# A step planner that models the VectorE/GpSimd exclusion and the one holder of a PSUM bank, and cos(h) from one biased Sin

## The chip, the cores and the metric

The kernel runs on one core of one Trainium2 chip. The metric is the device time of one execution in microseconds (us), the median of the runs shown. The core has five engines that work side by side and wait for each other through semaphores: TensorE (PE in the rows, its weight loads PEld), VectorE (DVE), ScalarE (ACT), GpSimd (POOL) and SyncE (SP, which issues DMAs here). Each engine runs its own queue strictly in the order in which the program was written out.

## What is computed

The reference runs three stages on 3072 tokens of width 384 (8 heads of 48, 4 batches of 768 steps):

```python
for t in range(S):                                  # linear attention with a decayed state
    kt, vt, rt = k[:, :, t], v[:, :, t], r[:, :, t]
    cur = einsum('bhd,bhe->bhde', u[None] * kt, vt)
    y[:, :, t] = einsum('bhd,bhde->bhe', rt, state + cur)
    state = w[None, :, :, None] * state + einsum('bhd,bhe->bhde', kt, vt)
h = x @ w_in; x = (h * cos(h)) @ w_out              # dense MLP, d_ff 2048
skip = x @ w_skip > 0; e = argmax(x @ w_gate)       # 8 experts, the best one of each token
x[skip] += gate * (relu(x @ w1[e]) @ w2[e])
```

## The kernel before

The recurrence is cut into 12 chunks c of 64 steps, and each chunk into two halves h of 4 heads. All large products are made of float16 pairs (a high and a low part, three matmuls for one product), so that every operand has to be split on the elementwise engines. The program is a list of some 2,300 steps; each step is a few instructions on one engine and has a name such as `("cg", g, f)`. The names used below:

- **Attention of half (c, h).** GpSimd and VectorE prepare it: `km`, `rm` (times decay), `k1l`, `r1l`, `vl`, `knl`, `al`, `zl` (low parts, a subtraction of two SBUF tiles), `pr1`, `pr2`, `am` (the diagonal). VectorE copies the parts into block matrices: `k1b`, `vb`, `knb`, `zb`, two float16 copies each (L242). PE runs `A` (scores, 24 matmuls into `ps_a`), `Y` (output, 48 into `ps_y`) and `U` (state product, 24 into `ps_u`, which VectorE reads in `zu`).
- **Dense MLP of group g** (the 256 tokens of chunk g). `("G1", g, f)`, f = 0 to 7: 18 matmuls into one of three banks `ps_h`. Then a chain over one tile `s` of 128x512: `cn` on ScalarE (L799: h/2π rounded to an integer), `cr` on VectorE (L803: h minus that many turns), `cs` on ScalarE (L806: Sin of half the rest), `cq` (a square: on ScalarE at L813 in 83 of 96 cases, on GpSimd or VectorE at L815 in the 13 others), `cg` on VectorE (L819: (1/2 - square) times h), `ch` on ScalarE (high part) and `cl` on GpSimd (L824: low part). `("G2", g, t, q)`: 12 matmuls each into `ps_o`, for two token tiles t and four quarters q.
- **Routing of group g.** `lg` on VectorE reads the logits out of `ps_o` (L864), `ra` on VectorE makes the one-hot choice (L904 to L917, eight small instructions, the last of which writes `oh`), `rp` on PE counts (5 matmuls into `ps_u`), `rb` on VectorE makes the slot of each token (L938 to L946), `rs` on GpSimd stores the records by two indirect DMAs (L952).
- **Experts** at the end: `ws` loads, `eh2`/`el2` splits of the weights, `e1`, `e2` on PE, a gather and a scatter by GpSimd.

`ps_u` is one PSUM bank. It is used by `U`, by `rp`, by `clp` (a count at the end of group 9) and by `ovp`, and each of them has to leave it to its reader first.

The order of each engine's queue comes from the class `Plan`. `order()` plays the steps through greedy engines: at each moment an idle engine takes, among its steps whose inputs are there, the one with the lowest priority number. `add(key, engine, cost, fn, deps, prio)` gives the cost in ns (functions `c_a`, `c_v`, `c_p`), and the table `SHIFT` moves priorities of the first chunks. Only the order of the queues comes out of it; on the chip every instruction waits for its data. In this model VectorE and GpSimd never disturb each other, and the bank `ps_u` is not known to it. The step `rp` therefore carries two hand-written predecessors, `("zu", g + 2, 0)` and `("U", g + 2, 0)`.

Of the kernel before, what the change touches and what calls it, by code (L numbers as in the profile page):

```python
# [7 lines left out]
F32 = mybir.dt.float32  # L8
# [10 lines left out]
C = 64                  # chunk of the recurrence  # L19
NC = S // C             # chunks  # L20
KF = DFF // 128         # tiles of moe_d_ff
CAP = 256               # token slots of an expert outside of the overflow loop
NS = E * CAP // 128     # slot tiles
NOV = 24                # upper bound on overflow blocks
REC = 10                # words of a routing record: row of xd, row of the output, shifted logits
BIG = 1 << 20           # an id past every bound
NO = DM + 9
EARLY = [0, 2]          # slot tiles that take tokens of the groups up to GE only
GE = 9
TURN = [1, 3]           # slot tiles that the tensor engine transposes  # L30
TR = NT + 128           # records of an expert: its tokens, and those that closing a tile passes over
NF = 1                  # chunks whose attention is in float32 products
NXG = 7                 # gathered token tiles on chip
NWS = 4                 # loads of expert weights in flight

# powers of two that the float16 parts are scaled by
SR = 2.0 ** 7           # r times its decay
SK = 2.0 ** 7           # k times its decay
SA = SR * SK            # attention scores
SV = 2.0 ** 7  # L40
SKN = 2.0 ** 7          # k times its decay, for the state
SZ = SKN * SV           # state
SY = SA * SV            # = SZ * SR
# [4 lines left out]
SO = SH * SWO / 2       # cos(h) / 2 = 1 / 2 - sin(h / 2)^2  # L48
# [8 lines left out]
CF = {}                 # columns of the float constants  # L57
# [8 lines left out]
class Plan:  # L66
    """Lists single-engine steps in the order in which greedy engines would start them.

    A step has an estimate of its time, the steps it has to come after, and a priority (the lowest goes first).
    The order decides only what each engine's queue looks like; Tile waits for the data itself.  # L70
    """
# [3 lines left out]
    SELF = {"PE": 0, "V": 125, "A": 140, "P": 100}  # L75

# [6 lines left out]

    def order(self):
        left, users = {}, {}
        for k, (_, _, _, deps, _, _) in self.steps.items():
            deps = [d for d in deps if d in self.steps]
            left[k] = len(deps)
            for d in deps:
                users.setdefault(d, []).append(k)  # L90
        done, ring, rings, heat = {}, 0.0, [], 0.0
        engs = ("PE", "V", "A", "P", "Q", "N")
        ready, free = {e: [] for e in engs}, {e: self.START + 400 * (e == "A") for e in engs}
        seq = {k: i for i, k in enumerate(self.steps)}
# [4 lines left out]
        while any(ready.values()):  # L99
            at, eng = min((max(free[e], min(r for r, _ in ready[e])), i) for i, e in enumerate(engs) if ready[e])  # L100
            eng = engs[eng]
            _, _, pick = min((self.steps[k][4], seq[k], (r, k)) for r, k in ready[eng] if r <= at)
            ready[eng].remove(pick)
            k = pick[1]
            _, cost, _, _, _, nbytes = self.steps[k]
# [8 lines left out]
            if nbytes:  # L114
                # at most 8 DMAs are under way
# [11 lines left out]
            else:  # L127
                end = at + cost + self.LAT.get(eng, 0)
                free[eng] = at + cost
            out.append((at, len(out), k))  # L130
            done[k] = end, free[eng]
            for u in users.get(k, ()):
                left[u] -= 1
                if not left[u]:
# [3 lines left out]
                    ready[eu].append((t, u))  # L138
# [7 lines left out]


# The start, where the elementwise engines carry the most: shifts of priorities, the order of the pieces of w_in and
# w_out, and steps on another engine than usual.
PIECES = "iiioioioioioiooo"  # L150
PIECE_0, PIECE_STEP = -40, 8
SHIFT = {
# [1269 lines left out]
```

## Time and profile before

| | us |
|---|---|
| runs | 777.3, 778.96, 1282.4 (median 778.96) |
| the profiled execution's span | 781.2 |
| PE busy in it | 628.7 |
| DVE busy in it | 613.4 |
| ACT busy in it | 438.7 |
| POOL busy in it | 430.1 |

The steps are recorded by helpers, so a line such as L236 (every matmul) or L242 (every VectorE copy) stands for many steps, and tiles tell them apart. A matmul's row lasts longer than its share of the queue, since matmuls overlap. A VectorE or GpSimd row begins when the instruction leaves the queue: what it waits for after that is inside its duration. Waits for semaphores are shown as idle time before a row, in square brackets, with the row that ended it. For the profiled execution, the routing steps `rp` of groups 0 to 8 stand at 169.3, 220.2, 270.6, 323.2, 370.4, 416.9, 462.7, 506.0 and 545.1 us; they serve as milestones.

### The profile page before, as it was taken

Reading aid. Unit: us, or ns where it says so; the run is one execution under the profiler, and the core shown is the slowest. Engines: PE = TensorE matmul, PEld = TensorE weight load, DVE = VectorE, ACT = ScalarE, POOL = GpSimd, SP = SyncE. Lnnn points to the kernel's source line nnn. Section 1 sums busy time; section 2 is a strip of 40 time slices with the busy share of each in tenths; the row PEclk is TensorE's granted clock in tenths of the full one; section 3 lists DMA queues with packets and bytes.
Section 4 is the critical chain, followed back from the end, with each engine's and each line's share of the span. In section 5 each row is a group of like instructions: output and inputs, shape, how many; then the busy total and the mean of one; then the engine's idle time right before and its main releaser. Section 6 shows DMA issues by size and latency. Waiting matters only on the chain. (4 is left out here: it accounts for less than half of the span.)

```text
span 781.2 us, 16117 instructions
## 1 busy us (share of the span) xinstructions
PE 628.7 (80%) x6407; PEld 477.6 (61%) x6407; DVE 613.4 (79%) x1022; ACT 438.7 (56%) x743; POOL 430.1 (55%) x367
## 2 busy tenths in 40 slices
PE   3436578958779497696996969799998998998994
PEld 3434456737557375474774748577775576675672
DVE  7999999998889989787886878776576537987641
ACT  3356667777654545464655645666676524655420
POOL 6787878468777766766566666442334424222110
PEclk9998799989989799698998989999999999999997
DMA  9867535440213203122120311201077224999610
GB/s 248 241 157 219 136 81 141 132 129 24 81 52 103 76 4 108 45 68 88 46 91 21 111 44 57 76 1 47 13 239 233 71 57 112 265 293 270 222 37 16
DMA packets 64752, 86.95 MB, mean 111 GB/s; under 512 B 32878, under 2 KB 49436, under 8 KB 64674
## 3 DMA queue, kind: packets, MB, share of 16 engines
q1 hardware_dynamic: 61570, 80.56, 36.0%
q0 software_dynamic: 2816, 4.91, 2.3%
q8 instruction: 51, 0.84, 0.5%
q10 hardware_dynamic: 288, 0.43, 0.2%
q14 instruction: 27, 0.22, 0.1%
HBM read 66.57 MB, written 13.73 MB: 103 GB/s over the span
## 5 line engine op out<-in xcount | busy, mean ns | idle before, releaser
L236 PE MATMUL ps_h<-xt,wih 128*128 128x256 f16 x1152 | 210.5, 287 | 20.1 <-DVE s L819 20.1
L236 PE MATMUL ps_o<-wo,gt 128*128 128x393 f16 (+2 forms) x1200 | 209.1, 326 | 0.1
L824 POOL TENSOR_TENSOR gt<-s,gt 128x512 f16<-128x512 f32 x96 | 121.0, 1264 | 106.8 <-ACT gt L240 106.0
L236 PE MATMUL ps_h<-xt,wil 128*128 128x256 f16 x576 | 165.1, 287 | 0.0
L236 PEld LDWEIGHTS <-gt 128*128 128x128 f16 x1200 | 113.5, 99 | 73.9 <-issue 3.0
L236 PEld LDWEIGHTS <-wih 128*128 128x128 f16 x1152 | 114.0, 102 | 45.0 <-DVE s L819 19.5
L819 DVE SCALAR_TENSOR_TENSOR s<-s,ps_h 128x512 f32<-128x512 f32 x96 | 65.3, 682 | 44.2 <-ACT s L813 43.6
L803 DVE SCALAR_TENSOR_TENSOR s<-s,ps_h 128x512 f32<-128x512 int32 x96 | 65.3, 681 | 29.7 <-ACT s L799 29.5
L806 ACT ACTIVATE s<-s 128x512 f32<-128x512 f32 x96 | 60.3, 628 | 49.9 <-DVE s L803 48.7
L240 ACT ACTIVATE gt<-s 128x512 f16<-128x512 f32 x96 | 60.0, 626 | 46.2 <-DVE s L819 45.8
L236 PE MATMUL ps_o<-w,hh 128*128 128x384 f16 x384 | 67.5, 332 | 4.8 <-ACT hh L1187 2.7
L799 ACT ACTIVATE s<-ps_h 128x512 int32<-128x512 f32 x96 | 56.3, 586 | 24.3 <-PE ps_h L236 23.6
L247 DVE SCALAR_TENSOR_TENSOR w<-ws,w 128x768 f16<-128x768 f32 (+1 forms) x56 | 59.4, 1076 | 11.6 <-ACT w L240 10.5
L240 ACT ACTIVATE w<-ws 128x768 f16<-128x768 f32 (+1 forms) x56 | 51.3, 930 | 29.6 <-DMA ws<-in_w_dram 19.2
L236 PE MATMUL ps_h<-xe,w 128*128 128x256 f16 (+1 forms) x720 | 65.7, 251 | 2.6 <-issue 1.7
L236 PEld LDWEIGHTS <-wil 128*128 128x128 f16 x576 | 59.4, 103 | 9.6
L236 PEld LDWEIGHTS <-w 128*128 128x128 f16 x720 | 58.9, 98 | 9.1 <-issue 3.1
L1220 POOL DMA_INDIRECT out_dram<-xg,recs x16 | 19.0, 1185 | 72.6 <-DVE xg L1215 52.9
L236 PEld LDWEIGHTS <-hh 128*128 128x128 f16 x384 | 37.1, 99 | 32.0 <-DVE hh L1192 4.2
L952 POOL DMA_INDIRECT tab<-rec,di x24 | 25.6, 1065 | 51.3 <-DVE osum L946 27.9
L813 ACT ACTIVATE s<-s 128x512 f32<-128x512 f32 x83 | 52.1, 627 | 2.1
L236 PE MATMUL ps_u<-oh,tri 128*128 128x8 f16 x24 | 2.9, 174 | 58.8 <-DVE oh L917 58.8
(179 smaller groups left out, 1193.9 us busy)
## 6 DMA issues: line engine op xcount, KB each, us to landing
nat<-in_nat_dram SPq DMA_DIRECT2D x24, 576.0 KB, 3.8
ws<-in_w_dram SPq DMA_DIRECT2D x24, 512.0 KB, 4.4
ws<-in_w_dram SPq DMA_DIRECT2D x32, 384.0 KB, 3.7
rk<-in_rk_dram SPq DMA_DIRECT2D x24, 448.0 KB, 3.7
so<-in_w_out_dram SPq DMA_DIRECT2D x8, 768.0 KB, 8.5
si<-in_w_in_dram SPq DMA_DIRECT2D x8, 576.0 KB, 6.9
xd<-y SPq DMA_DIRECT2D x24, 192.0 KB, 2.0
out_dram<-y SPq DMA_DIRECT2D x48, 96.0 KB, 2.2
```

What stands on the lines that cost most here:

```text
L236: T.matmul(o, lhsT=l, rhs=r, start=start, stop=stop)
L240: A.activation(out=o, in_=i, func=AF.Copy, scale=scale)
L247: V.scalar_tensor_tensor(out=o, in0=x, scalar=scale, in1=hi, op0=ALU.mult, op1=ALU.subtract)
L799: A.activation(out=n, in_=d["ph"], func=AF.Copy, scale=1.0 / (TWO_PI * SH))
L803: V.scalar_tensor_tensor(out=d["s"], in0=d.pop("n"), scalar=-TWO_PI * SH, in1=d["ph"], op0=ALU.mult, op1=ALU.add)
L806: lambda: A.activation(out=d["s"], in_=d["s"], func=AF.Sin, scale=0.5 / SH), [("cr", g, f)], pr)
L813: A.activation(out=d["s"], in_=d["s"], func=AF.Square)
L819: V.scalar_tensor_tensor(out=d["s"], in0=d["s"], scalar=0.5, in1=d.pop("ph"), op0=ALU.subtract, op1=ALU.mult, reverse0=True)
L824: lambda: P.tensor_tensor(out=gt[g][1][:, 2 * f:2 * f + 2], in0=d.pop("s"), in1=gt[g][0][:, 2 * f:2 * f + 2], op=ALU.subtract), [("ch", g, ...
L952: P.indirect_dma_start(out=tab[:, :], out_offset=bass.IndirectOffsetOnAxis(ap=di[:, t], axis=0), in_=rec[:, t], in_offset=None, bounds_che ...
L1220: P.indirect_dma_start(out=out[:, :], out_offset=bass.IndirectOffsetOnAxis(ap=xo["recs"][:, s, 1:2], axis=0), in_=xs_.pop(s), in_offset=No ...
```

## The change

Every comment and docstring is dropped, which moves the line numbers. Three things change.

First, the planner. A step of VectorE that reads two SBUF tiles (or copies float16 inside SBUF) is listed in `SHARED`; it and every step of GpSimd hold a common port, one at a time. While the port is held, such a step's priority is worsened by 0.04 per ns of waiting. Steps that take the bank `ps_u` (`TAKES`) are set aside while another one holds it, until its reader has run. In return `rp` and `clp` lose their hand-written predecessors. Costs of the float16 copies get a formula of their own, `c_cp`.

Second, cos(h) is computed as sin(h - 2πn + π/2), with n = round(h/2π + 1/4). The step `cq` is gone: 83 instructions of ScalarE, 8 of GpSimd, 5 of VectorE. `cn` and `cs` get a bias, and `cg` multiplies by 1/2 and by h in the same single instruction.

Third, as all priorities and costs go through the new planner, the queues of all five engines come out in another order. The tables `SHIFT`, `ENGINE` and `PIECES` are left as they were.

```diff
+    SHARED = {"wu": 1, "wx": 1, "wv": 1, "wl": 1, "k1b": 2, "k1l": 1, "r1l": 1, "pr1": 1, "pr2": 1, "am": 1, "vl": 1,
+              "vb": 2, "knm": 1, "knl": 1, "knb": 2, "al": 1, "zl": 1, "zb": 2, "us": 1, "tabs": 10, "tkd": 4, "ra": 8,
+              "rb": 3, "el2": 1, "cq": 1, "km": 2, "rm": 1}
+    WAIT = 0.04
+    TAKES = {"U": "zu", "rp": "rb", "clp": "clv", "ovp": "ov0"}
...
-            _, _, pick = min((self.steps[k][4], seq[k], (r, k)) for r, k in ready[eng] if r <= at)
+            busy = max(0.0, port.get(eng, 0.0) - at)
+            _, _, pick = min((self.steps[k][4] + (self.WAIT * busy if self.shared(k, eng) else 0.0), seq[k], (r, k))
+                             for r, k in ready[eng] if r <= at)
             ready[eng].remove(pick)
             k = pick[1]
+            if self.takes(k):
+                held = True
+                parked += [x for x in ready["PE"] if self.takes(x[1])]
+                ready["PE"] = [x for x in ready["PE"] if not self.takes(x[1])]
...
-                end = at + cost + self.LAT.get(eng, 0)
-                free[eng] = at + cost
+                n = self.shared(k, eng)
+                if n:
+                    start = max(at, port[eng])
+                    port["P" if eng == "V" else "V"] = free[eng] = start + cost
+                else:
+                    free[eng] = at + cost
+                end = free[eng] + self.LAT.get(eng, 0)
             out.append((at, len(out), k))
             done[k] = end, free[eng]
+            if self.gives(k):
+                held = False
+                ready["PE"] += [(max(r, end), x) for r, x in parked]
+                parked = []
...
+def c_cp(n):
+    return 171 + n * 0.26
...
-            k1e, cost = pick("k1b", "V", V=2 * c_v(2 * nk, 4), A=2 * c_a(2 * nk))
+            k1e, cost = pick("k1b", "V", V=2 * c_cp(2 * nk), A=2 * c_a(2 * nk))
...
-        cb = {"A": 2 * c_a(2 * nd), "V": 2 * c_v(2 * nd, 4)}
+        cb = {"A": 2 * c_a(2 * nd), "V": 2 * c_cp(2 * nd)}
...
-            A.activation(out=n, in_=d["ph"], func=AF.Copy, scale=1.0 / (TWO_PI * SH))
+            A.activation(out=n, in_=d["ph"], func=AF.Copy, scale=1.0 / (TWO_PI * SH), bias=0.25)
...
-            lambda: A.activation(out=d["s"], in_=d["s"], func=AF.Sin, scale=0.5 / SH), [("cr", g, f)], pr)
+            lambda: A.activation(out=d["s"], in_=d["s"], func=AF.Sin, scale=1.0 / SH, bias=math.pi / 2), [("cr", g, f)], pr)
-        qe, cost = "A", c_a(512) + 140
-        if g < 3:
-            qe, cost = on(("cq", g, f), "A", A=cost, P=c_p(512), V=c_v(512))
...
-        add(("cq", g, f), qe, cost, fn, [("cs", g, f)], pr)
-        def fn():
-            V.scalar_tensor_tensor(out=d["s"], in0=d["s"], scalar=0.5, in1=d.pop("ph"),
-                                   op0=ALU.subtract, op1=ALU.mult, reverse0=True)
-        add(("cg", g, f), "V", c_v(512), fn, [("cq", g, f)], pr)
+            V.scalar_tensor_tensor(out=d["s"], in0=d["s"], scalar=0.5, in1=d.pop("ph"), op0=ALU.mult, op1=ALU.mult)
+        add(("cg", g, f), "V", c_v(512), fn, [("cs", g, f)], pr)
...
-        used = [("zu", g + 2, 0), ("U", g + 2, 0)]
         add(rkey("rp", j), "PE", 100, fn,
-            [rkey("ra", j), rkey("rb", j - 1), "cst16", "tabi", "clv" if g == GE + 1 else None] + used, pr)
+            [rkey("ra", j), rkey("rb", j - 1), "cst16", "tabi", "clv" if g == GE + 1 else None], pr)
```

What that does to the queues is shown at three places, all around the routing of group 4.

**TensorE, ahead of `rp` of group 4.** Between the last `G2` matmul of group 4 and this `rp` stood `G1` of (6, 0) and `A` of (7, 0). The rows before are the end of that `A` and the beginning of `rp`:

```order
L236 LDWEIGHTS k1bd_83
L236 MATMUL ps_a<-r_3677,k1bd_83 128x64
L236 LDWEIGHTS tri
L236 MATMUL ps_u<-oh,tri 128x8
L236 LDWEIGHTS ones
L236 MATMUL ps_u<-osum,ones 128x8
```

And now:

```order
L282 LDWEIGHTS wil
L282 MATMUL ps_h<-xt,wil 128x256
L282 LDWEIGHTS tri
L282 MATMUL ps_u<-oh,tri 128x8
L282 LDWEIGHTS ones
L282 MATMUL ps_u<-osum,ones 128x8
```

The `rp` has moved behind two more `G1` steps and a `G2` quarter: 18 `ps_h`, 12 `ps_o` and 18 `ps_h` matmuls more stand between the logits' last matmul and it. Behind it, three `G2` quarters (36 matmuls) now stand ahead of `U` of (7, 0).

**VectorE, up to the one-hot `oh` of group 4.** The rows before (`s` is the tile of the cosine, `lg` the logits):

```order
L803 SCALAR_TENSOR_TENSOR s_4443<-s_4443,ps_h_4399 128x512
L819 SCALAR_TENSOR_TENSOR s_4443<-s_4443,ps_h_4399 128x512
L803 SCALAR_TENSOR_TENSOR s_4491<-s_4491,ps_h_4452 128x512
L819 SCALAR_TENSOR_TENSOR s_4491<-s_4491,ps_h_4452 128x512
L864 TENSOR_SCALAR lg_4307<-ps_o_4372 128x9
L588 TENSOR_REDUCE cc_4445<-pr_4337 128x8
L904 TENSOR_REDUCE mx_4538<-lg_4307 128x2
L907 TENSOR_TENSOR rec_4540<-lg_4307,mx_4538 128x2x8
```

And now:

```order
L288 COPY k1bd0_83<-k1d_4309 48x16x64 x2
L900 TENSOR_SCALAR lg_4143<-ps_o_3995 128x9
L850 SCALAR_TENSOR_TENSOR s_4355<-s_4355,ps_h_4313 128x512
L288 COPY vbd0_87<-vd_4010 64x16x48 x2
L856 SCALAR_TENSOR_TENSOR s_4355<-s_4355,ps_h_4313 128x512
L596 TENSOR_TENSOR zd_4340<-zs_91,zd_4340 112x384
L634 TENSOR_REDUCE cc_4468<-pr_4365 128x8
L288 COPY zbd1_90<-zd_4340 48x16x48 x2
L940 TENSOR_REDUCE mx_4491<-lg_4143 128x2
L943 TENSOR_TENSOR rec_4493<-lg_4143,mx_4491 128x2x8
```

The last two pairs of `cr` and `cg` of the group stood back to back ahead of the logits; now one pair stands behind them, with copies of the attention in the gap. Six copies and low parts come between the logits and the routing.

**GpSimd, behind the record stores `rs` of group 4.** Before, and then now:

```order
L952 DMA tab_69<-rec_4540,di_4617 25600x10 x2
L824 TENSOR_TENSOR gt1_4513<-s_4583,gt0_4512 128x512
L550 TENSOR_TENSOR am_4722<-cfs_71,cc_4445 128x512
L824 TENSOR_TENSOR gt1_4513<-s_4643,gt0_4512 128x512
L550 TENSOR_TENSOR k1d_4700<-rk_4195,k1d_4700 112x512
```

```order
L986 DMA tab_69<-rec_4493,di_4555 25600x10 x2
L596 TENSOR_TENSOR k1d_4572<-rk_3947,k1d_4572 112x512
L860 TENSOR_TENSOR gt1_3744<-s_4223,gt0_3743 128x512
L596 TENSOR_TENSOR pr_4721<-nat_4184 128x384
L860 TENSOR_TENSOR gt1_3744<-s_4355,gt0_3743 128x512
```

Before, GpSimd prepared half (8, 1) there (`k1d`); now it prepares (7, 1), half a dozen PE steps ahead of the scores that use it, and still has the cosine tiles of group 5's last pieces (`gt1_3744`) to do.

## Rows read from the trace of the kernel before

**Rows 1.** First part of the page: engine, busy us, share of span, instructions.

```profile
PE 628.7 (80%) x6407; PEld 477.6 (61%) x6407; DVE 613.4 (79%) x1022; ACT 438.7 (56%) x743; POOL 430.1 (55%) x367
```

**Rows 2.** Waits of PE: who waited for whom, us in total, times, longest.

```profile
PE ps_u L236 <- DVE oh L917: 58.8, 8, 9.6
PE ps_h L236 <- DVE s L819: 20.1, 14, 3.3
```

**Rows 3.** Stretches: length, busy us PE, PEld, DVE, ACT, POOL, clock, DMA share, GB/s.

```profile
0.00:169.30 169.30, 98.31 (x1102) 82.65 (x1102) 164.71 (x200) 100.22 (x162) 121.60 (x93) 0.93 0.62 165
169.30:545.10 375.80, 317.30 (x3497) 240.26 (x3497) 307.48 (x533) 221.04 (x395) 241.11 (x211) 0.92 0.21 62
220.20:270.60 50.40, 39.29 (x439) 29.84 (x439) 46.43 (x71) 27.81 (x51) 37.53 (x34) 0.91 0.24 77
506.00:545.10 39.10, 39.09 (x438) 29.85 (x438) 27.63 (x60) 24.94 (x44) 14.62 (x13) 0.96 0.10 27
545.10:632.10 87.00, 82.25 (x702) 58.27 (x699) 50.87 (x112) 53.18 (x89) 32.22 (x32) 1.00 0.41 131
632.10:781.20 149.10, 130.83 (x1115) 96.41 (x1112) 90.35 (x178) 64.30 (x99) 35.19 (x31) 0.96 0.58 164
```

**Rows 4.** Timeline of PE around `rp` of group 4: start us, us, instructions, [idle before].

```profile
362.68 0.27 PE L236 MATMUL ps_h<-xt,wil 128*128 128x256 f16 x1
...
370.42 0.19 PE L236 MATMUL ps_u<-oh,tri 128*128 128x8 f16 x1 [6.77 <-DVE oh L917]
...
370.95 0.42 PE L236 MATMUL ps_h<-xt,wil 128*128 128x256 f16 x1
```

**Rows 5.** Timeline of DVE in the same stretch.

```profile
366.59 0.69 DVE L819 SCALAR_TENSOR_TENSOR s<-s,ps_h 128x512 f32<-128x512 f32 x1 [1.36 <-ACT s L813]
367.19 0.16 DVE L864 TENSOR_SCALAR lg<-ps_o 128x9 f32<-128x9 f32 x1
...
367.92 1.61 DVE L907 TENSOR_TENSOR rec<-lg,mx 128x16 f32<-128x16 f32 x1
...
370.19 0.17 DVE L917 TENSOR_TENSOR oh<-eq,do 128x16 f16<-128x16 f32 x1
```

**Rows 6.** Timeline of POOL in the same stretch.

```profile
367.11 1.28 POOL L550 TENSOR_TENSOR rk<-rk,tr 112x512 f32<-112x512 f32 x1
368.34 1.17 POOL L824 TENSOR_TENSOR gt<-s,gt 128x512 f16<-128x512 f32 x1
```

**Rows 7.** Lines L242, L550, L579, L247, L907 on DVE: count, ns min/median/max, first and last start.

```profile
L242 DVE COPY zbd<-zd x40: 342/357/3182, 34.0 to 533.9; 48x768 f16<-48x768 f16 x40
L242 DVE COPY k1bd<-k1d x38: 406/1026/3864, 43.1 to 519.8; 48x1024 f16<-48x1024 f16 x38
L242 DVE COPY knbd<-knd x28: 339/1156/2587, 203.9 to 496.3; 64x768 f16<-64x768 f16 x28
L550 DVE TENSOR_TENSOR ah<-am,ah x18: 683/693/2636, 69.1 to 552.3; 128x512 f16<-128x512 f32 x18
L550 DVE TENSOR_TENSOR zd<-zs,zd x17: 542/547/1514, 138.0 to 532.4; 112x384 f16<-112x384 f32 x17
L579 DVE TENSOR_TENSOR r<-rk,r x16: 693/1158/4303, 191.2 to 520.8; 112x512 f16<-112x512 f32 x16
L247 DVE SCALAR_TENSOR_TENSOR vd<-nat,vd x22: 541/552/2240, 49.5 to 531.9; 128x384 f16<-128x384 f32 x22
L907 DVE TENSOR_TENSOR rec<-lg,mx x13: 167/202/1611, 168.3 to 632.7; 128x16 f32<-128x16 f32 x11, 128x8 f32<-128x8 f32 x2
```

**Rows 8.** Squares: L815 by stretch (DVE, POOL us), L813, and the wait for it.

```profile
0.00:169.30 169.30, 2.66 (x2) 4.16 (x4) 0.93 0.62 165
169.30:545.10 375.80, 4.22 (x3) 4.18 (x4) 0.92 0.21 62
L813 ACT ACTIVATE s<-s x83: 612/630/636, 75.2 to 615.0; 128x512 f32<-128x512 f32 x83
DVE s L819 <- ACT s L813: 43.6, 36, 1.7
```

More of the change, by code (lines that the diff above doesn't have):

```diff
@@ L82, in add, with shared, takes, gives @@
         self.steps[key] = (eng, cost, fn, [d for d in deps if d is not None], prio + SHIFT.get(group(key), 0), nbytes)
+    def shared(self, key, eng):
+        if eng == "P":
+            return 1
+        return self.SHARED.get(key[0] if isinstance(key, tuple) else key, 0) if eng == "V" else 0
+    def takes(self, key):
+        return (key[0] if isinstance(key, tuple) else key) in self.TAKES
+    def gives(self, key):
+        return (key[0] if isinstance(key, tuple) else key) in self.TAKES.values()
     def order(self):
         left, users = {}, {}
+        held, parked = False, []
         for k, (_, _, _, deps, _, _) in self.steps.items():
@@ L93, in order @@
         ready, free = {e: [] for e in engs}, {e: self.START + 400 * (e == "A") for e in engs}
+        port = {"V": 0.0, "P": 0.0}
         seq = {k: i for i, k in enumerate(self.steps)}
@@ L137, in order @@
                             else done[d][0] for d in self.steps[u][3] if d in self.steps)
-                    ready[eu].append((t, u))
+                    if held and self.takes(u):
+                        parked.append((t, u))
+                    else:
+                        ready[eu].append((t, u))
         stuck = [k for k in self.steps if k not in done]
@@ L805, in mlp1 @@
         add(("cs", g, f), "A", c_a(512),
-            lambda: A.activation(out=d["s"], in_=d["s"], func=AF.Sin, scale=0.5 / SH), [("cr", g, f)], pr)
-        qe, cost = "A", c_a(512) + 140
-        if g < 3:
-            qe, cost = on(("cq", g, f), "A", A=cost, P=c_p(512), V=c_v(512))
+            lambda: A.activation(out=d["s"], in_=d["s"], func=AF.Sin, scale=1.0 / SH, bias=math.pi / 2), [("cr", g, f)], pr)
         def fn():
-            if qe == "A":
-                A.activation(out=d["s"], in_=d["s"], func=AF.Square)
-            else:
-                ENG[qe].tensor_tensor(out=d["s"], in0=d["s"], in1=d["s"], op=ALU.mult)
-        add(("cq", g, f), qe, cost, fn, [("cs", g, f)], pr)
-        def fn():
-            V.scalar_tensor_tensor(out=d["s"], in0=d["s"], scalar=0.5, in1=d.pop("ph"),
-                                   op0=ALU.subtract, op1=ALU.mult, reverse0=True)
-        add(("cg", g, f), "V", c_v(512), fn, [("cq", g, f)], pr)
+            V.scalar_tensor_tensor(out=d["s"], in0=d["s"], scalar=0.5, in1=d.pop("ph"), op0=ALU.mult, op1=ALU.mult)
+        add(("cg", g, f), "V", c_v(512), fn, [("cs", g, f)], pr)
         add(("ch", g, f), "A", c_a(512), lambda: copy(A, gt[g][0][:, 2 * f:2 * f + 2], d["s"]), [("cg", g, f)], pr)
@@ L964, in fn @@
             mm(p, ones, osum, True, True)
-        c = min(GE + 2, NC - 2)
-        add("clp", "PE", 50, fn, [("rb", GE), ("zu", c, 0), ("U", c, 0)], 100 * (GE + 1) + 11)
+        add("clp", "PE", 50, fn, [("rb", GE)], 100 * (GE + 1) + 11)
         def fn():
```

## The prediction, made before the changed kernel ran

> **What bounds the kernel now.** The shares on the page come first: PE is busy 80% and DVE 79% of the span, POOL 55% and ACT 56% [rows 1]. These are averages, so I read the waits of PE next: 58.8 us go to eight waits of one kind, up to 9.6 us each, in which `rp` waits for the one-hot `oh` of VectorE [rows 2]. The only other sizeable kind is 20.1 us in which a `G1` waits for its bank until `cg` (L819) has read it. Then I cut the span at the `rp` steps [rows 3]. Three stages appear. Up to 169.3 us DVE is busy 164.7 us: the start is bound by the elementwise engines. From 169.3 to 545.1 eight groups pass in 375.8 us, 47.0 us each; neither PE (317.3) nor DVE (307.5) is full. From 545.1 on, PE is busy 82.3 of 87.0 and then 130.8 of 149.1 us: bound by PE.
>
> In the middle stage two figures set limits. The last group, 506.0 to 545.1, has PE busy for all of its 39.1 us and no wait for `oh`: that is a group's cost on PE. The other is a port that VectorE and GpSimd share. The VectorE instruction L907 took 1.61 us where 0.17 is its shortest [rows 5, 7]; it began while POOL was in the middle of a product and ended at 369.53, just after POOL's next product (368.34 + 1.17 = 369.51) [rows 6]. The copies show the same: 339 to 406 ns at best, up to 3864 [rows 7]. So such an instruction stands still while POOL works.
>
> What a group needs of this port, taking the shortest durations: four instructions each of the copies `knb`, `k1b`, `zb` and `vb` (the last like `zb`), 4 x (0.34 + 0.41 + 0.34 + 0.34) = 5.7 us; two each of `r1l`, `vl`, `al`, `zl`, 2 x (0.69 + 0.54 + 0.68 + 0.54) = 4.9 us; 11 small routing instructions at 0.17, 1.9 us [rows 7]. That is 12.5 us for VectorE. POOL is busy 241.1 us in the eight groups [rows 3], 30.1 each. The port therefore needs 42.6 of 47.0 us, 91%, against PE's 39.1. That the port can be filled is seen from 220.2 to 270.6: 37.5 + 12.5 = 50.0 of 50.4 us. So PE's waits for `oh` are the symptom. Behind them stand the port and an order that was made without it: `oh` is late because `lg` waits behind cosine pairs, each of which waits for ScalarE (1.36 us in the row), and then L907 waits for POOL [rows 5].
>
> **The squares.** They go: on ACT 83 x 0.63 = 52.3 us [rows 8], but ACT is busy 221.0 of 375.8 us in the middle [rows 3], so this is worth nothing as work. It shortens the cosine chain by 0.63 us, and VectorE waited 43.6 us for its end [rows 8]; that time becomes idle time of VectorE only if nothing else stands in the queue, and the port is still to be paid. I cost it at zero; if the port were not the limit, it would give up to those 43.6 us to VectorE. On the port, POOL's squares take 4.16 us before 169.3 us and 4.18 us after it; VectorE's two before and three after took 2.66 and 4.22 us with their waits [rows 8], and at 0.69 each, the shortest of another 512-column subtraction [rows 7], 1.4 and 2.1 us. So the port gains 5.5 us in the start and 6.3 us in the middle. The bias of `cn` and `cs` adds no instruction; no row shows a biased ACTIVATE. Below, nothing; above, another 0.63 us in each of 96 chains on ACT, which has the room. I take nothing.
>
> **The new order.** In group 4, `rp` stood behind one `G1` and one `A`, and waited 6.77 us [rows 4]. Now two `G1` steps and a `G2` quarter more stand ahead of it. A group's 39.1 us on PE hold 16 such steps and the attention's six, so one is at most 39.1 / 16 = 2.4 us; I take 2.1, and so 6.3 us of cover more. On VectorE the way from `lg` to `oh` now holds a cosine pair (1.4 us), four copies (1.4), `zl` and `cc` (1.1, both taken as `zl`) and the eight routing instructions (1.4), 5.3 us without waits. Cover and way are of a size, so most of the 58.8 us goes; what stays depends on port waits, a few us per group at most. After a wait a `ps_h` matmul takes 0.42 us where it took 0.27, and the clock of the middle stage is 0.92 [rows 3, 4]: PE runs some us after each wait at 1.2 instead of 2.4 GHz, which also goes when the wait does.
>
> What is late next is the port. All steps of it stay, less the squares: 42.6 - 6.3 / 8 = 41.8 us per group, if POOL's work is spread evenly instead of being done two chunks ahead (in the last group POOL is busy only 14.6 of 39.1 us, having worked ahead). Perfect packing is unlikely on queues that were planned with estimates, so I take 42.4. Eight groups: 8 x (47.0 - 42.4) = 36.8 us. The start gives 4 of its 5.5 us of squares; its order changes wholesale with tables of priorities left as they were, which I bound by ten us either way and take as zero. After 545.1 PE is the limit and its work is the same: zero. DMA issues move with their steps on SP and POOL: loads of the next chunk wait for the release of their one buffer, and DMA is busy 21% in the middle [rows 3], so I cost them nothing; without that cover POOL's `km` would wait for its load.
>
> Sum: 781.2 - 36.8 - 4 = 740.4 us of span. The median of the runs is 2.2 us below the profiled span; I say 740.
>
> **A rule beside it.** The Trainium skill, page "SBUF — State Buffer", section "SBUF: two separate sides", says that VectorE in a two-port mode or with two SBUF inputs and GpSimd take a shared pair of ports as an exclusive lock, for a whole instruction, and that the one that starts first blocks the other. The trace agrees on the blocking (1.61 against 0.17 us), but its row shows a wait that goes on through a second GpSimd product. By the page no wait is longer than one GpSimd instruction; by the rows a copy can lose 2.2 or even 3.5 us.
>
> **Rivals.** *PE alone decides.* The rows of VectorE's waits shrink once the order fits, POOL's own waits (it is blocked too) go as well, and a group costs PE's 39.1: 8 x (47.0 - 39.1) = 63.2, less 4: 714, or 712 as a median. For it: POOL's 241.1 us include its own waiting. Against: 41.8 of port work. 0.15.
>
> *The waits only change place.* The new order is as imprecise as the old; VectorE stays as long in port waits as now, and only the squares on the port count: 4 + 6.3 = 10.3, so 771, or 769. For it: the planner's costs are short of the rows (a 512-column step of VectorE counts 68 + 512 x 1.042 = 601 ns in it, and takes 0.69 us [rows 5]), so that the queues drift from any plan. Against: `rp` has 6.3 us more cover, which holds whatever drifts. 0.20.
>
> *Slower: `U` waits in place of `rp`.* `U` uses the bank after `rb` and needs `knb`, which VectorE now has right behind `rb`. On PE 36 `ps_o` matmuls, three quarters or 6.3 us, stand between `rp` and `U`; VectorE needs for `cr`, `vl`, `rb` and the pair of copies 0.7 + 0.5 + 1.2 + 0.7 = 3.1 us at best, and each copy can take 2587 - 339 = 2.25 us longer [rows 7]. If both halves pay that in full, beyond what the cover holds, each group loses 4 x 2.25 = 9.0 us and a rest of 1 at `rp`: 39.1 + 10.0 = 49.1 instead of 47.0, 8 x 2.1 = 17 us, less 4 from the start: 794, or 792. It decides from 7.9 us of waits per group on. Against: the median copy is 1156 ns, far under that, and one half has a slack of 3.2 us. 0.15. By the page's rule a copy waits for one product, about 1.3 us; then the four cost 5.2 us, and this rival ends below 47.0.
>
> **How the numbers follow.** My forecast, the port, has 0.50, and 723 to 757 as its own range (781.2 - 2.2 less 8 x 5.2 and 14 at 41.8 us per group with a start ten us better; less 8 x 3.5, plus 6, at 43.5 with one ten us worse). The others have 0.15, 0.20 and 0.15. The range reaches down to PE's 712, rounded to 710, and up to 782, where only most of the slower case and a little below PE's limit are left out. A measurement of this kernel tells 2% from no change: faster means under 763. The forecast and PE's case are faster (0.65), the third within 2% (0.20), the last slower (0.15).
>
> **What would show it.** In the changed kernel's waits of PE, the kind `ps_u` for `oh` should fall from 58.8 to under 20 us, and the `rp` milestones should lie about 42 us apart; POOL and VectorE's port work should fill over 95% of that. If the kind is gone but the milestones lie 47 apart, look for `U`, `A` or `Y` waiting for copies (the third or the fourth case); if they lie 39 apart, PE decided. Wrong at the root would be a start that takes clearly longer than 169 us to the first `rp`, or a stage behind 545 that grows because expert weights come late.

## The result, and the profile after

The changed kernel takes 751.7 us (median; 748.1 to 753.7), the kernel before 781.2 us beside it (with a fourth run, of 783.35 us). The ratio is 0.962, 95% interval 0.958 to 0.967: 3.8% faster, some 29 us, where 41 were forecast. A median below is of all runs of a kernel, while a ratio leaves out its runs that are over 1.5% above its fastest, so that the two can differ (port_only). The profiled execution has a span of 750.8 us.

First part of the page of the changed kernel, as in [rows 1] (engine, busy us, share of the span, instructions):

```profile
PE 630.7 (84%) x6407; PEld 479.0 (64%) x6407; DVE 609.9 (81%) x1017; ACT 386.4 (51%) x660; POOL 420.9 (56%) x359
```

ScalarE is busy 52.3 us less, the time of its squares; GpSimd (9.2 us) and VectorE (3.5 us) lost a few squares too, and PE does the same work. The waits of PE, as in [rows 2]:

```profile
PE ps_o L282 <- DMA wt<-wo: 18.4, 13, 5.7
PE ps_y L282 <- DVE ah L596: 14.4, 6, 4.1
...
PE ps_h L282 <- DVE s L856: 10.7, 6, 6.1
PE ps_a L282 <- DVE am L709: 10.0, 1, 10.0
...
PE ps_u L282 <- DVE oh L953: 1.6, 2, 1.1
```

The wait for the one-hot `oh` has fallen from 58.8 to 1.6 us. The largest kind now lies in the start (`wt`: transposed pieces of w_out); waits for `ah`, the split scores, are new. The `rp` steps of groups 0 to 8 now stand at 171.8, 204.7, 259.3, 299.4, 337.0, 380.1, 423.0, 468.3 and 513.4 us. Busy time by stretch, cut at the first and at the ninth of them, as in [rows 3]:

```profile
0.00:171.80 171.80, 107.72 (x1036) 85.44 (x1037) 148.50 (x191) 93.01 (x149) 113.20 (x89) 0.88 0.60 155
171.80:513.40 341.60, 314.61 (x3611) 243.21 (x3610) 310.75 (x531) 187.04 (x342) 231.77 (x201) 0.98 0.24 72
513.40:750.80 237.40, 208.33 (x1763) 150.37 (x1761) 150.69 (x295) 106.34 (x171) 75.97 (x70) 0.97 0.52 150
```

| stage | before | after | change | forecast |
|---|---|---|---|---|
| start, to `rp` of group 0 | 169.3 | 171.8 | +2.5 | -4 |
| eight groups, to `rp` of group 8 | 375.8 | 341.6 | -34.2 | -36.8 |
| the rest | 236.1 | 237.4 | +1.3 | 0 |
| span | 781.2 | 750.8 | -30.4 | -40.8 |

The milestone moved a little in PE's own queue: 66 matmuls fewer stand ahead of the first `rp`, 114 more between the first and the ninth. The start is therefore worse than it looks, and the middle better. A stage of a single profile is not sharp, either: five runs shown below in which the order up to the ninth `rp` is the same (pool_extra, dve_extra, pe_less, no_copies, late_xn) have the start at 167.3 to 172.5 us, and the first four of them, whose order is the same to the end, have the rest at 235.5 to 239.9. So +2.5 and +1.3 cannot be told from zero; that the start gained nothing, with less of PE's work done, stands.

In the middle VectorE was idle for 375.8 - 307.5 = 68.3 us; now it is idle for 341.6 - 310.8 = 30.9 us. The stage became shorter by 34.2 us, and VectorE's idle time by 37.4. PE's idle time fell as well, from 375.8 - 317.3 = 58.5 to 341.6 - 314.6 = 27.0 us. These sums say which idle time went, not what made it go. Two groups of the page of the changed kernel show where VectorE's idling went (busy us, mean ns; then idle us before the instruction and what ended it):

```profile
L856 DVE SCALAR_TENSOR_TENSOR s<-s,ps_h 128x512 f32<-128x512 f32 x96 | 64.9, 680 | 10.0 <-ACT s L853 9.1
L850 DVE SCALAR_TENSOR_TENSOR s<-s,ps_h 128x512 f32<-128x512 int32 x96 | 64.4, 680 | 5.0 <-ACT s L846 4.2
```

VectorE waited 43.6 us in `cg` for ScalarE's part of the cosine [rows 8]; now 9.1. Its waits in that chain in the middle stage alone, in `cg` and in `cr`, before and then after (us in total, times, longest):

```profile
DVE s L819 <- ACT s L813: 34.9, 27, 1.7
DVE s L803 <- ACT s L799: 21.1, 21, 2.4
```

```profile
DVE s L856 <- ACT s L853: 3.1, 6, 1.0
DVE s L850 <- ACT s L846: 0.6, 1, 0.6
```

The timeline of VectorE up to `rp` of group 4 shows how, as [rows 5] did before:

```profile
328.77 0.17 DVE L900 TENSOR_SCALAR lg<-ps_o 128x9 f32<-128x9 f32 x1
328.97 0.69 DVE L850 SCALAR_TENSOR_TENSOR s<-s,ps_h 128x512 f32<-128x512 int32 x1
329.58 0.72 DVE L288 COPY vbd<-vd 64x768 f16<-64x768 f16 x2
330.36 0.69 DVE L856 SCALAR_TENSOR_TENSOR s<-s,ps_h 128x512 f32<-128x512 f32 x1
...
331.89 1.46 DVE L288 COPY zbd<-zd 48x768 f16<-48x768 f16 x2
...
334.20 1.20 DVE L946 SCALAR_TENSOR_TENSOR eq<-rec,cfs 128x16 f32<-128x16 f32 x1
...
336.72 0.17 DVE L953 TENSOR_TENSOR oh<-eq,do 128x16 f16<-128x16 f32 x1
```

No row has an idle time before it: between `cr` (L850) and `cg` (L856) of one tile stand two copies instead of a wait. From `lg` to `oh` it is now 8.0 us, where it was 3.0 [rows 5]: more stands in between, and some of the rows wait for GpSimd (1.20 us where 0.17 is the shortest). PE does not feel it: its row of this `rp` reads

```profile
336.95 0.17 PE L282 MATMUL ps_u<-oh,tri 128*128 128x8 f16 x1 [1.06 <-DVE oh L953]
```

against 6.77 us of wait [rows 4]. Why not, PE's own queue says. The last matmul that the logits of group 4 need ends these two rows, before and after:

```profile
356.80 4.18 PE L236 MATMUL ps_o<-wo,gt 128*128 128x393 f16 x24
```

```profile
324.77 2.51 PE L282 MATMUL ps_o<-wo,gt 128*128 128x393 f16 x14
```

From there to the end of `oh` it was 9.4 us (360.98 to 370.36), and now it is 9.6 (327.28 to 336.89), so VectorE is no sooner. But 42 matmuls stood between that matmul and `rp`, and now there are 90. In the traces it was 42 in each of the nine groups before, and it is 48 to 180 now. Over groups 0 to 7 the way from that matmul to the end of `oh` is 10.8 us on average before and 8.9 after, and PE's own work covers 3.5 us of it before and 9.9 after. The wait is gone because `rp` stands further back, behind work that PE can do meanwhile.

What did not shrink much are the waits for the shared port themselves. All of VectorE's copies (L242 before, L288 after) in the middle stage, before and after (length, busy us, instructions, clock):

```profile
169.30:545.10 375.80, 88.70 (x116) 0.92 0.21 62
171.80:513.40 341.60, 82.22 (x116) 0.98 0.24 72
```

At 0.34 to 0.41 us each, 116 copies would take 41 us [rows 7]. Over all of VectorE's instructions in the stage, the time above the shortest row of the same operation, tiles and shape was 92 us before and is 101 now. So, as far as these rows tell, a planner that knows the port has not made the two engines meet less. What came out of it is another order: VectorE has other work while ScalarE is busy, and PE has other work while VectorE makes `oh`.

### The profile page after: what moved, and what is told of

It reads as the page before. It is cut to its first block, busy times and chain, and to the rows that moved or that the text cites. A ratio compares the mean times of both kernels' runs of the same rounds, so it can differ in the third digit from the quotient of the medians.

```text
span 750.8 us, 16041 instructions
## 1 busy us (share of the span) xinstructions
PE 630.7 (84%) x6407; PEld 479.0 (64%) x6407; DVE 609.9 (81%) x1017; ACT 386.4 (51%) x660; POOL 420.9 (56%) x359
## 5 line engine op out<-in xcount | busy, mean ns | idle before, releaser
L282 PE MATMUL ps_h<-xt,wih 128*128 128x256 f16 x1152 | 208.0, 286 | 14.6 <-DVE s L856 10.7
L282 PE MATMUL ps_o<-wo,gt 128*128 128x393 f16 (+2 forms) x1200 | 204.4, 324 | 0.0
L860 POOL TENSOR_TENSOR gt<-s,gt 128x512 f16<-128x512 f32 x96 | 126.2, 1323 | 68.4 <-ACT gt L286 64.0
L282 PEld LDWEIGHTS <-gt 128*128 128x128 f16 x1200 | 111.8, 98 | 73.1 <-issue 0.5
L853 ACT ACTIVATE s<-s 128x512 f32<-128x512 f32 x96 | 59.6, 624 | 30.5 <-DVE s L850 30.1
L293 DVE SCALAR_TENSOR_TENSOR w<-ws,w 128x768 f16<-128x768 f32 (+1 forms) x56 | 62.3, 1134 | 15.2 <-ACT w L286 12.2
L856 DVE SCALAR_TENSOR_TENSOR s<-s,ps_h 128x512 f32<-128x512 f32 x96 | 64.9, 680 | 10.0 <-ACT s L853 9.1
L850 DVE SCALAR_TENSOR_TENSOR s<-s,ps_h 128x512 f32<-128x512 int32 x96 | 64.4, 680 | 5.0 <-ACT s L846 4.2
L286 ACT ACTIVATE w<-ws 128x768 f16<-128x768 f32 (+1 forms) x56 | 51.0, 930 | 28.7 <-DMA ws<-in_w_dram 22.9
L986 POOL DMA_INDIRECT tab<-rec,di x24 | 24.7, 1029 | 55.2 <-DVE osum L980 30.4
L596 POOL TENSOR_TENSOR am<-cfs,cc 128x512 f32<-128x512 f32 x21 | 25.3, 1203 | 47.4 <-DVE cc L634 47.2
L282 PE MATMUL ps_y<-ah,vbd 128*128 128x64 f16 x528 | 38.4, 201 | 14.5 <-DVE ah L596 14.4
```

Source lines behind the costliest of these rows:

```text
L282: T.matmul(o, lhsT=l, rhs=r, start=start, stop=stop)
L286: A.activation(out=o, in_=i, func=AF.Copy, scale=scale)
L293: V.scalar_tensor_tensor(out=o, in0=x, scalar=scale, in1=hi, op0=ALU.mult, op1=ALU.subtract)
L596: do(name, e, cost, lambda: ENG[e].tensor_tensor(out=o(), in0=a(), in1=b(), op=op), deps, pr)
L850: V.scalar_tensor_tensor(out=d["s"], in0=d.pop("n"), scalar=-TWO_PI * SH, in1=d["ph"], op0=ALU.mult, op1=ALU.add)
L853: lambda: A.activation(out=d["s"], in_=d["s"], func=AF.Sin, scale=1.0 / SH, bias=math.pi / 2), [("cr", g, f)], pr)
```

## The experiments

The theory is that of the prediction: VectorE and GpSimd with their shared port set the pace, and the new order fills them. The rivals: the shorter cosine; the bank rule alone; PE. One more rival was not run: that `rp` only had to move back in PE's queue, with VectorE's order left as it was. Ratios are to the kernel before, each run beside it.

| kernel | us | ratio, 95% interval |
|---|---|---|
| the changed kernel | 751.7 | 0.962 (0.958 to 0.967) |
| cos_only | 782.5 | 0.998 (0.995 to 1.002) |
| planner_only | 768.9 | 0.985 (0.979 to 0.990) |
| bank_only | 777.2 | 0.995 (0.992 to 0.998) |
| port_only | 754.1 | 0.956 (0.950 to 0.962) |
| pool_extra | 769.1 | 0.989 (0.982 to 0.995) |
| dve_extra | 765.3 | 0.979 (0.973 to 0.985) |
| pe_less | 743.0 | 0.952 (0.948 to 0.957) |
| no_copies | 741.7 | 0.951 (0.947 to 0.955) |
| copies_act | 751.0 | 0.962 (0.956 to 0.968) |
| measured | 751.4 | 0.962 (0.957 to 0.967) |
| late_xn | 742.9 | 0.951 (0.945 to 0.957) |
| no_shift | 739.9 | 0.946 (0.939 to 0.953) |

### Which part of the change does it

**cos_only**: the kernel before with the cosine's lines of the change, among them these (the line of `cg` changes as in the diff above).

```diff
-  A.activation(out=n, in_=d["ph"], func=AF.Copy, scale=1.0 / (TWO_PI * SH))
+  A.activation(out=n, in_=d["ph"], func=AF.Copy, scale=1.0 / (TWO_PI * SH), bias=0.25)
-  ... func=AF.Sin, scale=0.5 / SH)
+  ... func=AF.Sin, scale=1.0 / SH, bias=math.pi / 2)
-  add(("cq", g, f), qe, cost, fn, [("cs", g, f)], pr)
```

> The kernel before with its own planner, and the new cosine alone (no square, biased Sin). The theory of the prediction (the port that VectorE and GpSimd share sets the pace, and the new order fills it) expects about 771 us, 766 to 776: only the 11.8 us of squares on the port, and the waits of PE for the one-hot of the routing still near 55 us. A rival (the cosine chain is what counts, since VectorE waited 43.6 us for its squares) expects 755 us or less.

**planner_only**: the changed kernel with the lines shown under cos_only turned back to those of the kernel before; the planner stays the new one.

> The changed kernel with the old cosine (square and unbiased Sin back), everything else as changed. The port theory expects about 762 us, 757 to 768: the order keeps its gain, the squares come back on the port. The chain rival expects 775 us or more.

**bank_only**: the changed kernel, whose planner does not know the port.

```diff
     def shared(self, key, eng):
-        if eng == "P":
-            return 1
+        return 0
```

> The changed kernel, but its planner lets VectorE and GpSimd run side by side as the old one did; the rule of the one holder of the bank and the new cosine stay. The port theory expects 765 to 775 us, little better than the cosine alone, with PE still waiting over 40 us for the one-hot. A rival (the routing count only had to lose its two hand-written predecessors) expects 750 to 758 us, as the changed kernel.

**port_only**: the changed kernel, whose planner does not know the bank (`clp` gets its two predecessors back as well).

```diff
-    TAKES = {"U": "zu", "rp": "rb", "clp": "clv", "ovp": "ov0"}
+    TAKES = {}
...
-            [rkey("ra", j), ..., "clv" if g == GE + 1 else None], pr)
+            [rkey("ra", j), ..., "clv" if g == GE + 1 else None, ("zu", g + 2, 0), ("U", g + 2, 0)], pr)
```

> The changed kernel, but without the bank rule: the two hand-written predecessors of the routing count are back, the planner still models the shared port. The port theory expects 750 to 758 us, as the changed kernel. The rival of the bank rule expects 765 us or more.

The cosine alone changes nothing that can be measured, less even than the 10 us expected. The bank rule with the cosine comes to 0.995 (0.992 to 0.998), half a percent. Without the bank rule the kernel is as fast as with it: 0.956 against 0.962, with overlapping intervals. So the exclusion in the planner carries the change; with the old cosine it and the bank rule give 0.985. port_only lies within what was expected of it; planner_only (768.9 us) and bank_only (777.2) end one and two us above theirs, and cos_only 6.5 above. One row each from the waits of PE says why, of cos_only and then of bank_only:

```profile
PE ps_u L236 <- DVE oh L905: 52.9, 8, 7.9
```

```profile
PE ps_u L281 <- DVE oh L952: 51.3, 8, 9.0
```

In both, PE still waits for `oh` in eight groups, and in both the 42 matmuls of the kernel before stand ahead of `rp` from group 1 on. With the planner that knows the port the wait is nearly gone, with or without the bank rule (2.1 us in port_only, 6.8 in planner_only).

The two parts do not add up: 0.2% and 1.5% alone, 3.8% together. The shorter cosine is worth nothing in the old order and about 2.2%, 17 us, beside the new planner. That these 17 us are the work of the squares is not shown, since the planner makes another order with them than without. The middle stage of planner_only (to compare with the second row of the changed kernel above, and its instructions of PE, x3611):

```profile
187.30:520.60 333.30, 301.15 (x3374) 227.30 (x3373) 311.85 (x508) 201.32 (x371) 219.86 (x190) 0.98 0.23 69
```

Its first `rp` came 15.5 us later than that of the changed kernel. As the milestones cut it, the difference lies outside of the middle stage, which is shorter, with fewer matmuls in it; per matmul it is somewhat slower, 333.3 / 3374 = 99 ns against 341.6 / 3611 = 95 ns, though the mix of matmuls is not the same.

### What sets the pace now

Here the order of the changed kernel stays as it is, and work is added or left out inside steps of groups 2 to 9 or chunks 5 to 11.

**pool_extra** and **dve_extra**:

```diff
@@ pool_extra: behind the low part of the cosine, for 2 <= g <= 9 and even f
+                P.tensor_tensor(out=scr, in0=cfs[:, 0:384], in1=cfs[:, 0:384], op=ALU.mult)
@@ dve_extra: behind cg, for 2 <= g <= 9 and even f
+                for _ in range(2):
+                    V.tensor_reduce(out=sc1, in_=cfs[:, 0:320], axis=AX.X, op=ALU.add)
```

> The changed kernel with the order of its steps unchanged; GpSimd does one more product of two constant 128x384 tiles into a spare tile behind every second low part of the cosine in groups 2 to 9: 32 instructions of some 0.92 us, 29 us of the shared port. The port theory (331.8 of 341.6 us of the middle stage filled) expects 20 to 29 us more than the changed kernel, 772 to 781 us. A rival (PE sets the pace of the middle stage now) expects 6 us more or less.

> The changed kernel with its order unchanged; VectorE does two more sums over 320 constant columns (one SBUF input, some 0.48 us each, a kind that never waits for GpSimd) behind every second cosine product in groups 2 to 9: 64 instructions, 31 us of VectorE that are not on the port. The port theory expects at most 10 us more than the changed kernel, 750 to 762 us. A rival (VectorE as a whole, its work and its waits, busy 310.8 of 341.6 us, sets the pace) expects 20 to 30 us more.

**pe_less**:

```diff
                     mm(ph[:, q], wih[:, j, m], x[:, j, 0], j == 0, False)
-                    mm(ph[:, q], wih[:, j, m], x[:, j, 1], False, False)
+                    if not 2 <= g <= 9:
+                        mm(ph[:, q], wih[:, j, m], x[:, j, 1], False, False)
```

> The changed kernel with its order unchanged, but in groups 2 to 9 the first MLP product leaves out one of its three partial products (high weights times low part of x): 384 matmuls of 128x256 less, about 41 us of PE at the fast clock. The port theory expects 0 to 8 us less than the changed kernel, 743 to 752 us. The rival (PE sets the pace of the middle stage) expects 20 us less or more, 732 us at most.

**no_copies**:

```diff
-                for j, (_, ph, _) in enumerate(R2):
+                for j, (_, ph, _) in enumerate(R2 if c < 5 else ()):
                     copy(ENG[ve], vbd[h][ph, :, :, 48 * j:48 * j + 48], d["vd"][ph])
...
-                    for j, (_, ph, pc) in enumerate(R2):
+                    for j, (_, ph, pc) in enumerate(R2 if c < 5 else ()):
                         copy(ENG[kbe], knbd[h][ph, :, :, pc], d["knd"][ph])
```

> The changed kernel with its order unchanged, but the block copies of v and kn of chunks 5 to 11 are left out (52 instructions of VectorE; PE reads the blocks of chunk 4 in their place, so the output is another). That is 18 us of the port and, with their waits, 29 us of VectorE. If the work on VectorE and the port sets the pace of the middle stage, 10 to 18 us less than the changed kernel, 734 to 742 us. If the pace is set by the order itself (each engine waits for single results of the others, and freed time is not used), 4 us less at most, 747 us or more.

The middle stage of each, in the same order: pool_extra, dve_extra, pe_less, no_copies.

```profile
167.30:527.60 360.30, 322.11 (x3613) 247.28 (x3612) 327.99 (x531) 187.85 (x343) 258.98 (x233) 0.96 0.23 69
```

```profile
172.40:527.40 355.00, 320.87 (x3612) 246.27 (x3611) 325.46 (x595) 187.10 (x342) 230.02 (x201) 0.96 0.23 70
```

```profile
167.90:506.40 338.50, 289.66 (x3231) 213.48 (x3228) 308.35 (x533) 187.94 (x343) 234.68 (x202) 0.93 0.24 74
```

```profile
168.20:503.80 335.60, 312.89 (x3612) 241.26 (x3610) 276.04 (x481) 186.61 (x342) 231.38 (x201) 0.98 0.25 74
```

The whole times move by the differences of the ratios: GpSimd's 28.7 us of added work (32 instructions of 897 ns in its trace) cost 2.6%, 20 us; VectorE's 30.8 us outside of the port cost 1.7%, 13 us. PE's 41 us less gave 1.0%, 8 us. The copies left out gave 1.1%, 9 us: they were 18 us of the port at their shortest and took 29 us in the changed kernel, and VectorE is busy 34.7 us less.

So PE is not the limit, as predicted: only a fifth of what it is spared comes back, and its granted clock in the stage falls from 0.98 to 0.93. A row of the waits of PE in pe_less shows part of what takes the rest:

```profile
PE ps_u L282 <- DVE oh L954: 11.0, 5, 2.7
```

The order is that of the changed kernel, but PE's work ahead of `rp` is shorter, and the wait for `oh` is back at 11.0 us from 1.6. So it is this work that hides the way to `oh`.

Work added to the elementwise engines is paid for by two thirds on GpSimd and by two fifths on VectorE off the port; the first is at the lower end of its expectation (20 to 29 us more; as a time, 769.1 us, it misses 772), the second misses its own (at most 10 us) and does not reach the rival's (20). But the port as a full resource, in which each microsecond counts, is not what no_copies shows. There the stage fell by 6.0 us, from 42.7 to 42.0 us per group, while VectorE, at 276 of 336 us, had time to spare. By the ratios its 9 us miss both expectations (10 to 18, or 4 at most); the median, 741.7 us, lies at the upper end of the first (734 to 742). PE, busy 312.9 of 335.6 us, could have given 22.7 us more at most. As these runs read, the engines hold each other in turn: adding work to one shows up, freeing one shows the next. What the limit would be with less work on GpSimd was not tried.

**copies_act** moves the same copies to ScalarE and lets the planner make a new order.

```diff
-        ve, cost = pick("vb", "A" if c < 1 else "V", **(cb1 if plain else cb))
+        ve, cost = pick("vb", "A" if c < 1 or c > 4 else "V", **(cb1 if plain else cb))
...
-                kbe, cost = pick("knb", "V", **cb)
+                kbe, cost = pick("knb", "A" if c > 4 else "V", **cb)
```

> The changed kernel with the block copies of v and kn of chunks 5 to 11 on ScalarE instead of VectorE (their engine alone is changed; the order comes out anew). Of the port that is eight copies of 0.34 us in each of seven groups, 19 us, and of VectorE with waits more. The port theory expects 12 to 22 us less than the changed kernel, 730 to 740 us. A rival (elementwise time is short on every engine, ScalarE included, which gets some 7 us per group to its 23) expects 748 to 758 us.

It gained nothing, where the theory wanted 12 us at least. Two rows of its waits of PE:

```profile
PE ps_h L282 <- DVE s L856: 15.8, 6, 6.7
PE ps_a L282 <- DVE k1bd L288: 11.6, 5, 5.2
```

PE waits more for VectorE's results (10.7 and 3.0 us in the changed kernel), though VectorE has less to do. Whether that is the new order or ScalarE's added 41 us (busy 427.6 us against 386.4) this run cannot tell; no_copies, with the order kept and nothing added, shows that the move had at most some 9 us to give.

### Where the rest of the forecast went

**measured**: the planner's costs fitted to the rows.

```diff
 def c_a(n, psum=False):
-    return (52 if psum else 93) + n / 1.2
+    return 150 + n * 0.843 if psum else 190 + n * 0.858
...
 def c_v(n, fast=1):
-    return 68 + n * 1.042 / fast
+    return 140 + n * 1.06 / fast
```

> The changed kernel, whose planner gets costs of VectorE and ScalarE fitted to the rows (512 columns: 683 ns instead of 601 on VectorE, 629 instead of 520 on ScalarE, 582 instead of 479 from PSUM); the order comes out anew. If the gain that the prediction expected and that did not come was lost to planned times that are short of the real ones, 740 to 748 us; if the order does not depend on such differences, 748 to 756 us.

No gain: the ratio is the same. Its first `rp` came at 187.9 us, 16 us later than in the changed kernel, and its middle stage was shorter. In this run, at least, planned times that fall short of the real ones are not what is missing.

**no_shift**: the table of shifts for the first chunks is emptied.

```diff
-SHIFT = {
-    "ld_i0": -40, "w_i1": -300, "w_i2": -50, ...
-}
+SHIFT = {}
```

> The changed kernel with an empty table of priority shifts for the first chunks, which had been made for the old planner. If that table is why the start did not get shorter, the first routing count comes before 165 us and the time is 735 to 746 us; if it still helps, the time is 752 us or more and the first count comes after 172 us.

The time is that of the first expectation, 0.946, so 1.6% better than the changed kernel and the fastest of all. But the first `rp` came at 170.1 us, not before 165. The stretches of its profile say that the milestone hides it:

```profile
0.00:170.10 170.10, 105.39 (x1114) 84.65 (x1114) 152.13 (x192) 97.72 (x156) 116.69 (x92) 0.95 0.63 164
170.10:511.50 341.40, 318.02 (x3570) 242.43 (x3571) 315.44 (x531) 183.24 (x334) 230.53 (x200) 0.98 0.23 69
```

PE has done 1114 matmuls by then, where the changed kernel has done 1036 at 171.8 us and the kernel before 1102 at 169.3 us. So the start of the changed kernel had become slower, and without the table that had been made for the old planner PE gets as far in it as before the change. The middle stage is as long (341.4 us). The rest of the 1.6% lies at the end, 228.5 us behind the milestone against 237.4, with 37 matmuls fewer left to do there; which part of the new order gives it is open.

**late_xn**: a ScalarE step of the experts is held back.

```diff
-            add(("xeh", s), "A", c_a(DM), fn, [("ga", s), pb], xp)
+            add(("xeh", s), "A", c_a(DM), fn, [("ga", s), pb, ("cs", NC - 1, 5) if s in EARLY else None], xp)
```

> The changed kernel, but the first experts' token tiles are split on ScalarE only after the Sin of the last group's sixth piece, so that no Sin stands behind a step that waits for a gather. If the 6.1 us that PE waits at 562 us come from that, 745 to 749 us; if the wait only moves, 750 to 753 us.

In the changed kernel PE waited 6.14 us at 562 us. The timeline of ScalarE there:

```profile
560.73 0.84 ACT L286 ACTIVATE w<-ws 128x768 f16<-128x768 f32 x1 [2.21 <-DMA ws<-in_w_dram]
566.17 0.52 ACT L286 ACTIVATE xn<-xg 128x384 f16<-128x384 f32 x1 [4.60 <-DMA xg<-xd,recs]
566.60 0.61 ACT L853 ACTIVATE s<-s 128x512 f32<-128x512 f32 x1
```

The Sin for the last group stood behind `xn`, the split of gathered tokens, and `xn` waited 4.6 us for its gather. With `xn` later, PE's longest wait for the cosine falls from 6.1 to 2.1 us:

```profile
PE ps_h L282 <- DVE s L856: 6.3, 6, 2.1
```

The ratio is 0.951 (0.945 to 0.957) against 0.962 (0.958 to 0.967): about 8 us better, where 3 to 7 were expected, with intervals that all but touch. The profiled execution was the slowest of the five (750.3 us; the others 741.5 to 743.3), and its stage behind the ninth `rp` is 235.3 us against 237.4. The wait is shown to come from the gather; the size is not sharp.

## Why the prediction was right, and where not

*What bounds the kernel.* Right: the waits of PE for `oh` were a symptom. They went from 58.8 to 1.6 us, under the 20 that the prediction named as its sign, and the milestones lie 42.7 us apart, where it said about 42 (42.4 in the sum). By the prediction's own count the port is filled to (231.8 + 8 x 12.5) / 341.6 = 97%, over the 95% named. The reading that the port's sum is the floor of a group is weaker than this agreement suggests: with 18 us of it left out, only 6 us of the stage went, and the time above the shortest rows did not fall (92 and 101 us). That 42.7 came out beside 42.4 is in part luck. What the rows do show is the prediction's other step, the cover of `rp`, together with the end of VectorE's idling on the cosine chain, which the prediction had seen (1.36 us in the row) and gave no term. Both came with the same order, and no run has one without the other, so how the time divides between them is open.

*The squares.* As work on ScalarE they were worth nothing, as said; on the port they were costed at 5.5 and 6.3 us, of which 10.3 were taken. Alone they bring nothing, beside the new planner some 17 us. The prediction let them add to the order; the measured parts do not add up, and why is not shown.

*The new order, middle.* -36.8 forecast, -34.2 measured. The prediction took 6.3 us more of cover in group 4; the traces have 5.9 there (8.6 against 2.7) and 6.4 on average (9.9 against 3.5). This is what took the wait away, as said. The fourth case, `U` waiting for its copies, did not come: all waits of `U` for copies of `kn` on VectorE are 1.1 us.

*The start.* This term failed: -4 was taken, with ten us either way for the order, and +2.5 came, with less of PE's work done. The prediction read the start as bound by the elementwise engines. VectorE is busy 16.2 us less in it now (148.5 us against 164.7), and the first of the eight waits for `oh`, 9.0 us, stood at the end of the start and not in the middle:

```profile
169.32 0.19 PE L236 MATMUL ps_u<-oh,tri 128*128 128x8 f16 x1 [9.03 <-DVE oh L917]
```

It is gone too; yet the start is no shorter, and VectorE idles 23.3 us in it where it idled 4.6. In PE's rows 10.0 us are a new wait for `am`, and those for `wt` grew from 8.1 to 18.4 us. The prediction named the unchanged tables and took zero; no_shift shows that they cost time.

*The end.* Taken as zero, measured +1.3, which cannot be told from zero; in it a 6.1 us wait is new: a ScalarE step of the experts that waits for a gather ahead of the last Sin steps. The prediction looked at DMA issues as hidden and did not look for steps queued behind one that waits for a transfer.

*Rivals.* PE alone (0.15): no, pe_less gave a fifth of its work. Waits that only change place (0.20): no; some did (`ah`, 14.4 us), but not most. Its premise held, for VectorE is as long in such waits as before (92 and 101 us above the shortest rows); its price did not, because `rp` no longer stands behind them. The time lies in the forecast's own range, 723 to 757.

## What to carry to other kernels

When one engine waits in one place, ask two things: what the engine that it waits for was doing, and how much work of its own the waiting engine could do first. Here VectorE stood idle for 68 us, mostly behind a chain through ScalarE, and PE had 42 matmuls to do ahead of each wait. The new order changed both; the way to `oh` stayed about as long, and the contention did not fall. So a model in a planner can pay by the order that comes out, and not by what it models. Tables that were tuned for one scheduler are part of that scheduler: with the planner replaced, emptying the table was worth 1.6%. And parts of a change that make the order anew need not add up (0.2% and 1.5% alone, 3.8% together); time them together, not only alone.

## What the hardware showed that was not expected

A VectorE instruction that waits for the port is sometimes not let in between two GpSimd instructions that follow each other closely. In the kernel before, GpSimd's and VectorE's timelines around the longest wait:

```profile
262.54 0.99 POOL L550 TENSOR_TENSOR pr<-nat 128x384 f32<-128x384 f32 x1
263.50 1.15 POOL L824 TENSOR_TENSOR gt<-s,gt 128x512 f16<-128x512 f32 x1
264.61 0.98 POOL L550 TENSOR_TENSOR pr<-pr,cfs 128x384 f32<-128x384 f32 x1
265.56 0.98 POOL L550 TENSOR_TENSOR nat<-nat,tkn 128x384 f32<-128x384 f32 x1
```

```profile
262.79 4.30 DVE L579 TENSOR_TENSOR r<-rk,r 112x512 f16<-112x512 f32 x1
```

The subtraction takes 0.69 us alone [rows 7]. It began 0.25 us into the first of four GpSimd instructions, and ended 0.55 us after the last, 4.30 us in all. This is not the rule: in the kernel before, 127 of VectorE's rows overlap GpSimd's work and are over 0.25 us longer than the shortest of their kind; 98 of these waits end with the first GpSimd instruction, and 29 go on through two to four. Two rows of GpSimd in the changed kernel show the common case:

```profile
334.09 1.27 POOL L596 TENSOR_TENSOR rk<-rk,tk 112x512 f32<-112x512 f32 x1
335.33 1.26 POOL L596 TENSOR_TENSOR rk<-rk,tr 112x512 f32<-112x512 f32 x1
```

VectorE's row at 334.20 us (1.20 us, shown above) ended at 335.40, behind the first of them, though the second followed at once.

The Trainium skill's rule (page "SBUF — State Buffer", section "SBUF: two separate sides") is that the instruction that starts first holds the lock for its whole length and the other one blocks. The trace agrees for the 98 waits; that section does not say who comes next, and these rows show that the wait can last through four. So the prediction's reading, that by the Trainium skill no wait is longer than one GpSimd instruction, does not hold for the 29. The planner's model gives the port to VectorE after one. Which of the two will happen, the rows do not tell.
